# Units of 272 tokens per expert, with the second product transposed, in a fused attention, expert and GLU kernel

## The chip, the cores and the metric

The kernel runs on one core of a Trainium2 chip. The metric is the device time of one execution in microseconds (us). A core has a matrix engine (TensorE; its matmuls are the profile's PE, its weight loads PEld), a vector engine (VectorE, DVE), an activation engine (ScalarE, ACT), a general engine (GpSimd, POOL) and a queue that here only issues transfers (SyncE, SP). Each works through its own instructions in order, and semaphores make one wait for another.

## The reference

Attention inside chunks of 64 tokens, then a layer of eight experts, then a gated layer (GLU), on 4608 tokens of width 512:

```python
# attention: softmax(q k^T / 8) v in chunks of 64 tokens, giving x (4608 x 512)
do_compute = x @ w_skip > 0            # the other tokens pass unchanged
e_idx = argmax(x @ w_gate, axis=1)     # one expert per token
h = maximum(x[e] @ w1[e], 0)           # 512 -> 1024, per expert
x[e] += gate * (h @ w2[e])             # 1024 -> 512
out = (silu(x @ g_gate) * (x @ g_val)) @ g_out   # 512 -> 1536 -> 512
```

The inputs are drawn with seed 0. How many tokens go to each expert follows from them by the reference alone, without running the kernel:

| expert | 0 | 1 | 2 | 3 | 4 | 5 | 6 | 7 | sum |
|---|---|---|---|---|---|---|---|---|---|
| tokens | 271 | 252 | 388 | 506 | 104 | 266 | 237 | 266 | 2290 |
| of them among the first 3072 tokens | 206 | 125 | 257 | 435 | 77 | 191 | 163 | 232 | 1686 |

## The kernel before

Every float32 operand of a product is split into a high part and the rest, and a product is three matmuls that add up (`mm3`, L246 to L249: high by high, high by low, low by high). Weights are loaded by SP in halves of 512 KB (`st`, L134), four slices to a chunk. ACT rounds a slice to its high part (`whi`, L145), and DVE, or for each fourth slice POOL, subtracts (`wlo`, L147). Ten buffers hold five chunks of high and low parts. A unit of expert work needs four chunks.

**Slots.** While attention runs, the router gives each computed token a slot: expert number times 4608, plus its place among the tokens of that expert (L674 to L706). POOL scatters token number and gate to a table in DRAM, `perm`, at those slots (L709). A unit of work loads 128 entries of `perm` per tile of tokens (`pm`, L263), gathers the rows of X that they name (POOL, L276), and turns them for the matmuls on PE (`xpose`, L295 to L303).

**Static units** (`unit_static`) take the first UNIT = 256 slots of an expert. In eight steps over the hidden width, f = 0 to 7, the first product makes 128 hidden rows for 256 tokens (`hp`, weights stationary, 12 matmuls of 256 columns); ACT and DVE turn them into `hh` and `hl` (L351, L352); the second product of the step before adds to two tiles `y` (hidden rows stationary, weights moving, 6 matmuls of 512 columns). After step 7 `finish` (L308) computes x + gate * y.

**Dynamic units** (`unit_dyn`) take 128 further slots of whichever expert has them. Their place comes from a table `tab` that the kernel computes (`table`, L773 to L809): for each expert the tiles of 128 beyond UNIT slots, and their sum. NDYN = 7 of them stand in the program as written out code. If the sum is larger, a loop in the program (`For_i(NDYN, total, 1)`, L916 to L943) runs once for each further tile, with nothing else beside it. In the loop body SP loads `perm` and the four chunks of 1 MB, POOL gathers, and all 16 slices are split by ACT and POOL (L935, L936).

**The first unit** starts before routing is complete. It gathers only rows below 3072. So when the router has done the first 24 of 36 tiles of tokens (CUT, L693), it moves the counter of the first unit's expert up to UNIT if it is lower (`least`, L475): later tokens of that expert get slots from UNIT on. Before the change that expert is 0.

The order of the units is s0, s1, d0, s2, d1, ... s6, d5, s7, d6 with the last d5 and s7 exchanged (L118 to L121). The loop stands between the first unit and the second. All instructions are in an order written by hand: `tick(f)` (L955 to L985) issues, after step f of a unit, gathers, scatters, the turn of the next unit's rows and `pump` (splits of later weights). During static units it also prepares the first weights of the GLU (`gpump`, three DVE passes in L225 to L231).

Of the kernel before, what the change touches and what calls it, by code (L numbers as in the profile page):

```python
# [11 lines left out]
I32 = mybir.dt.int32  # L12
# [22 lines left out]
UNIT = 256  # L35
NDYN = NE - 1
# [14 lines left out]
def attention_moe_glu_kernel(  # L51
# [66 lines left out]
    units = [("s", 0)]  # L118
    for n in range(1, NE):
        units += [("s", n), ("d", n - 1)]  # L120
    units[-3:-1] = units[-2], units[-3]  # L121
# [151 lines left out]
    def gather(u, n=NT + 1):  # L273
        for r in rows[u]:
            x = al["x"](u)
            ins = nc.gpsimd.indirect_dma_start(  # L276
                out=x, out_offset=None, in_=X[0:n, :],
                in_offset=bass.IndirectOffsetOnAxis(ap=r[0][:, 0:1].bitcast(U32), axis=0),
                bounds_check=n - 1, oob_is_err=False,
            )  # L280
            apart(ins, u)
            r.append(x)


    def first_rows(u):
        rows[u] = []
        for t in range(2):
            x = al["x"](u)
            ins = nc.sync.dma_start(out=x, in_=X[t * P:(t + 1) * P, :])
            if not t:  # L290
                after(ins, [n for _, n in stored])
                stored.clear()
# [12 lines left out]
    def finish(u, ys):  # L305
        for (pm, x), y in zip(rows.pop(u), ys):
            o = al["o"](x)
# [16 lines left out]
    def unit_static(u, getc, donec, tail, tick, half=lambda f: None):  # L324
        xh, xl = xts.pop(u)
        ys = []

        def mm2(f, hh, hl):
            if f == 0:
                ys.extend(al["y"](t) for t in range(2))  # L330
            wh, wl = getc(2, f // 4)
            for t in range(2):
                ts = slice(t * P, (t + 1) * P)
                mm3(ys[t], hh[:, ts], hl[:, ts], wh[:, f % 4, :], wl[:, f % 4, :], f == 0, f == 7)
# [3 lines left out]
            if f == 7:  # L338
                finish(u, ys)

        for f in range(8):
# [13 lines left out]
            half(f)  # L355
            if tail:
                tail()
# [4 lines left out]
    def unit_dyn(u, getc, donec, tail, tick):  # L362
# [15 lines left out]
        def hpose(f2):  # L378
# [3 lines left out]
            hh = hp_[1].tile([P, 4, P], F32R, tag="hth", name="hth")  # L382
            hl = hp_[1].tile([P, 4, P], F32R, tag="htl", name="htl")
# [19 lines left out]
        if tail:  # L403
            tail()
        tick(0)
        mm1(1, (0, 1))
        tick(1)
# [11 lines left out]
    def pre_perm(u):  # L419
# [3 lines left out]
        if kind == "s":  # L423
            load_perm(u, [n * NT, n * NT + P])
# [7 lines left out]
    with ExitStack() as actx:  # L432
# [42 lines left out]
        nc.vector.memset(least[:, 0:1], float(UNIT))  # L475
# [242 lines left out]
        pm0 = [xtp.tile([P, 2], I32, name=f"pm{t}") for t in range(2)]  # L718
# [5 lines left out]
        for i in range(NTILE):  # L724
# [29 lines left out]
            if i == NTILE - 4:  # L754
                xs = x0p.tile([P, 2, DM], F32, name="x0")
                nc.gpsimd.memset(xs, 0.0)
                x0 = [xs[:, 0], xs[:, 1]]
            for n in range(2 if i < NTILE - LAG else len(pending)):
# [70 lines left out]
        def s0_tick(f):  # L829
# [17 lines left out]
            y=lambda t: ps_u.tile([P, DM], F32, tag="o", name="y"),  # L847
# [16 lines left out]
        around[0] = ps_u  # L864
        xt_p = ctx.enter_context(tc.tile_pool(name="xt", bufs=2, side="right"))
        mctx = ctx.enter_context(ExitStack())
        io = mctx.enter_context(tc.tile_pool(name="io", bufs=5, side="right"))
        hp_.append(mctx.enter_context(tc.tile_pool(name="h", bufs=3, side="right")))
# [19 lines left out]
        tail()  # L888
# [3 lines left out]
    with mctx:  # L892
# [57 lines left out]
        for u, (kind, n) in enumerate(units):  # L950
# [4 lines left out]
            def tick(f, u=u, kind=kind, nxt=nxt):  # L955
                if f == 1:
                    put()
                    if kind == "s":
                        gather(u + 1)
                if f == (5 if kind == "s" else 3) and nxt:  # L960
                    xpose(u + 1)
                if kind == "s":
# [7 lines left out]
                    if f == 6 and units[u + 1][0] == "d":  # L970
# [3 lines left out]
                if u == len(units) - 2 and f == 1:  # L974
# [26 lines left out]
    with ExitStack() as gctx:  # L1001
# [7 lines left out]
        sizes = [2, 2] + [BLK // P] * ((NT - 3 * UNIT) // BLK) + [2]  # L1009
# [140 lines left out]
```

## Time and profile before

| what | value |
|---|---|
| median of 3 runs | 1396.05 us (1394.64 to 1399.95) |
| the profiled execution | 1393.52 us |
| its span, first to last instruction | 1391.5 us |
| PE busy | 1314.6 us (94%) |
| DVE busy | 704.0 us (51%) |
| mean granted TensorE clock | 0.984 |

The span has four stretches: attention and routing with preparation to 161.1 us, the first unit and the check of the loop to 199.2 us, the other expert units to 473.2 us, and the GLU to the end. "Busy" of PE counts a matmul until its modelled end, and ends overlap the next start. The pace is therefore read from the distance of one start to the next. A row of the timeline gives the start, the duration, engine, line, operation, output and inputs, and what ended an idle time before it.

### The profile page before, as it was taken

To read this page: it belongs to the slowest core of one execution; us is meant where nothing else is said; L and a number is where in the kernel's file an instruction comes from. 1 tells how busy PE (TensorE), PEld (TensorE's weight loads), DVE (VectorE), ACT (ScalarE), POOL (GpSimd) and SP (SyncE) were. 2 spreads that over 40 slices of the span, in tenths; PEclk is the share of its full clock that TensorE was granted. 3 is DMA by queue.
4 is the path that set the end of the run, shared out by engine and by line. 5 is a ranking of instruction groups with operands and counts; after the bars stand their busy time and mean duration, and the time that the engine had idled before them with its cause. 6 is when DMAs were issued, how large, how long until landed. Compare 5 with 4: busy or idle time off the path is not lost.

```text
span 1391.5 us, 23406 instructions
## 1 busy us (share of the span) xinstructions
PE 1314.6 (94%) x9500; PEld 1190.1 (86%) x9500; DVE 704.0 (51%) x1207; ACT 450.7 (32%) x906; POOL 274.3 (20%) x233
## 2 busy tenths in 40 slices
PE   7766889999999899999999999999999999999998
PEld 6645678778778788999999999999999999999998
DVE  7755657998887788433332323333333333242322
ACT  4644435665665433311221212212121122121121
POOL 0333634555554466200000000000000000000000
PEclk9987989999999999999999999999999999999999
DMA  9998347888887745010202020201001020201000
GB/s 335 372 276 222 112 145 245 279 285 269 267 288 234 225 139 137 31 23 0 46 1 46 0 46 1 46 1 38 9 23 24 0 46 1 46 1 38 1 23 16
DMA packets 131855, 150.98 MB, mean 109 GB/s; under 512 B 78848, under 2 KB 79360, under 8 KB 131746
## 3 DMA queue, kind: packets, MB, share of 16 engines
q1 hardware_dynamic: 126914, 138.82, 32.6%
q0 software_dynamic: 4832, 10.65, 2.3%
q8 instruction: 75, 1.23, 0.4%
q14 instruction: 34, 0.28, 0.1%
HBM read 125.61 MB, written 25.28 MB: 108 GB/s over the span
## 4 chain that ended last, share of the span: by engine, by line
PE 69%; DVE 7%; issue 3%; DMA 2%; ACT 2%; POOL 2%; SPq 0%; DVEq 0%; ACTq 0%; POOLq 0%
PE o L249 7%; PE o L248 7%; PE o L247 7%; PE pg L249 6%; PE pg L247 6%; PE pg L248 6%; PE pv L247 6%; PE pv L248 6%; PE pv L249 6%; DVE wlo L147 3%; DMA st<-in_moe_w_dram 2%; ACT whi L145 2%; PE y L249 1%; PE y L247 1%; PE y L248 1%
## 5 line engine op out<-in xcount | busy, mean ns | idle before, releaser
L1091 DVE TENSOR_TENSOR sg<-pg,sg 128x384 f32<-128x384 f32 (+1 forms) x132 | 72.0, 546 | 327.0 <-ACT sg L1090 327.0
L1095 ACT ACTIVATE uh<-sg 128x384 fp32r<-128x384 f32 (+1 forms) x156 | 78.0, 500 | 311.8 <-DVE sg L1092 311.8
L249 PE MATMUL pg<-xh,glo 128*128 128x384 f32 (+1 forms) x528 | 175.7, 333 | 0.0
L247 PE MATMUL pg<-xh,ghi 128*128 128x384 f32 (+1 forms) x528 | 175.4, 332 | 0.0
L248 PE MATMUL pg<-xl,ghi 128*128 128x384 f32 (+1 forms) x528 | 175.0, 331 | 0.0
L247 PE MATMUL pv<-xh,ghi 128*128 128x384 f32 (+1 forms) x528 | 174.1, 330 | 0.0
L249 PE MATMUL pv<-xh,glo 128*128 128x384 f32 (+1 forms) x528 | 174.1, 330 | 0.0
L248 PE MATMUL pv<-xl,ghi 128*128 128x384 f32 (+1 forms) x528 | 174.1, 330 | 0.0
L249 PE MATMUL o<-ghi,ul 128*128 128x512 f32 x432 | 171.2, 396 | 2.2 <-POOL ul L1097 2.2
L247 PE MATMUL o<-ghi,uh 128*128 128x512 f32 x432 | 168.9, 391 | 2.6 <-ACT uh L1095 2.6
L248 PE MATMUL o<-glo,uh 128*128 128x512 f32 x432 | 170.8, 395 | 0.0
L1090 ACT ACTIVATE sg<-pg 128x384 f32<-128x384 f32 (+1 forms) x132 | 63.6, 482 | 312.7 <-PE pg L249 312.7
L147 DVE TENSOR_TENSOR wlo<-st,whi 128x512 fp32r<-128x512 f32 x165 | 151.0, 947 | 17.9 <-ACT whi L145 16.5
L145 ACT ACTIVATE whi<-st 128x512 fp32r<-128x512 f32 x240 | 137.7, 624 | 27.5 <-DMA st<-in_moe_w_dram 25.6
L147 POOL TENSOR_TENSOR wlo<-st,whi 128x512 fp32r<-128x512 f32 x75 | 101.4, 1352 | 156.4 <-ACT whi L145 142.0
L1092 DVE TENSOR_TENSOR sg<-pv,sg 128x384 f32<-128x384 f32 (+1 forms) x132 | 72.1, 546 | 118.6 <-PE pv L249 118.5
L1097 DVE TENSOR_TENSOR ul<-sg,uh 128x384 fp32r<-128x384 f32 (+1 forms) x132 | 72.2, 547 | 76.7 <-ACT uh L1095 76.7
L247 PEld LDWEIGHTS pg<-xh,ghi 128*128 128x128 f32 x528 | 99.5, 188 | 5.9
L248 PEld LDWEIGHTS pg<-xl,ghi 128*128 128x128 f32 x528 | 99.3, 188 | 5.7
L249 PEld LDWEIGHTS o<-ghi,ul 128*128 128x128 f32 x432 | 81.1, 188 | 21.6 <-POOL ul L1097 4.4
L249 PEld LDWEIGHTS pv<-xh,glo 128*128 128x128 f32 x528 | 99.4, 188 | 0.0
L248 PEld LDWEIGHTS pv<-xl,ghi 128*128 128x128 f32 x528 | 99.4, 188 | 0.0
(160 smaller groups left out, 2454.0 us busy)
## 6 DMA issues: line engine op xcount, KB each, us to landing
st<-in_moe_w_dram SPq DMA_DIRECT2D x120, 512.0 KB, 5.0
q<-in_qkv_dram SPq DMA_DIRECT2D x35, 768.0 KB, 9.8
X<-x SPq DMA_DIRECT2D x36, 256.0 KB, 9.7
out_dram<-os SPq DMA_DIRECT2D x36, 256.0 KB, 2.0
xr<-X SPq DMA_DIRECT2D x128, 64.0 KB, 2.6
gst<-in_moe_w_gate_dram SPq DMA_DIRECT2D x12, 512.0 KB, 4.1
gst<-in_moe_w_val_dram SPq DMA_DIRECT2D x12, 512.0 KB, 3.6
gst<-in_moe_w_out_dram SPq DMA_DIRECT2D x12, 512.0 KB, 3.7
```

The costliest lines, as they stand in the source:

```text
L145: nc.scalar.activation(out=hi[:, k, :], in_=stage[:, k % 2, :], func=ACTF.Copy)
L147: eng.tensor_tensor(out=lo[:, k, :], in0=stage[:, k % 2, :], in1=hi[:, k, :].bitcast(F32), op=ALU.subtract)
L247: nc.tensor.matmul(ps, ah, bh, start=start, stop=False)
L248: nc.tensor.matmul(ps, ah, bl, start=False, stop=False)
L249: nc.tensor.matmul(ps, al, bh, start=False, stop=stop)
L1090: nc.scalar.activation(out=u, in_=pg, func=ACTF.Sigmoid)
L1091: nc.vector.tensor_tensor(out=u, in0=pg, in1=u, op=ALU.mult)
L1092: nc.vector.tensor_tensor(out=u, in0=pv_, in1=u, op=ALU.mult)
L1095: nc.scalar.activation(out=uh, in_=u, func=ACTF.Copy)
L1097: eng.tensor_tensor(out=ul, in0=u, in1=uh.bitcast(F32), op=ALU.subtract)
```

## The change

A static unit has 272 slots: two tiles of 128 tokens and one of 16 (`rest`). The 16 rows of unit u lie in partitions from 32 * (u mod 4), and their table entries are loaded twice, once there and once at partition 0 as index for gather and scatter. The second product now has the weights stationary and the hidden rows moving: four tiles `yt` of 128 output columns by 272 tokens, 12 matmuls of 272 columns per step where there were 6 of 512. After the last step ACT copies the four tiles to `yts`, and in step 2 of the next unit PE turns them back in three groups (12 transposes, `turned`), after which `finish` adds into the gathered rows in place. For unit 0 this follows at once. The scatters move from tick 1 to tick 3 (tick 2 in a dynamic unit).

NDYN is 3. The order is expert 4 as first unit, then 0, 1, d0, 2, 3, 5, 6, 7, d1, d2; `least` holds for expert 4. Function and loop body of the dynamic units are the same, but for buffers. PSUM gives `yt` four single buffers, where `y` had two tiles of two buffers; the last of them also serves `y` of the dynamic units.

```diff
...
 RT = 4
-UNIT = 256
-NDYN = NE - 1
+UNIT = 272
+REST = UNIT - 2 * P
+FIRST = 4
+EXPERTS = [FIRST] + [e for e in range(NE) if e != FIRST]
+NDYN = 3
 TAB = 40
...
     ORDER_D = [(1, 0), (1, 1), (2, 0), (2, 1)]
-    units = [("s", 0)]
-    for n in range(1, NE):
-        units += [("s", n), ("d", n - 1)]
-    units[-3:-1] = units[-2], units[-3]
+    units = [("s", n) for n in EXPERTS]
+    for n, at in enumerate((3, 9, 10)):
+        units.insert(at, ("d", n))
     for kind, n in units:
...
+
+    def rest(u):
+        return slice(32 * (u % 4), 32 * (u % 4) + REST)
+
     def load_perm(u, bases):
         r = []
-        for b in bases:
+        for t, b in enumerate(bases):
             pm = al["pm"](u)
-            src = perm[b:b + P, :] if isinstance(b, int) else perm[bass.ds(b, P), :]
+            idx = pm
+            if t == 2:
+                src = perm[b:b + REST, :]
+                idx = al["pm"](u)[0:REST]
+                ins = nc.sync.dma_start(out=idx, in_=src)
+                after(ins, scattered)
+                pm = pm[rest(u)]
+            else:
+                src = perm[b:b + P, :] if isinstance(b, int) else perm[bass.ds(b, P), :]
             ins = nc.sync.dma_start(out=pm, in_=src)
             after(ins, scattered)
-            r.append([pm])
+            r.append([pm, idx])
         rows[u] = r
...
                 stored.clear()
-            rows[u].append([None, x])
+            rows[u].append([None, None, x])
...
         xh, xl = xts[u] = al["xt"](u)
-        for t, (_, x) in enumerate(rows[u]):
+        for t, (_, _, x) in enumerate(rows[u]):
             p = al["t"](t)
+            n = P
+            one = ident
+            if t == 2:
+                n = REST
+                one = ident[rest(u), rest(u)]
             for k in range(KD):
-                nc.tensor.transpose(p[:, k, :], x[:, k * P:(k + 1) * P], ident)
-            sl = slice(t * P, (t + 1) * P)
-            nc.scalar.activation(out=xh[:, :, sl], in_=p, func=ACTF.Copy)
-            nc.vector.tensor_tensor(out=xl[:, :, sl], in0=p, in1=xh[:, :, sl].bitcast(F32), op=ALU.subtract)
+                nc.tensor.transpose(p[:, k, 0:n], x[:, k * P:(k + 1) * P], one)
+            sl = slice(t * P, t * P + n)
+            nc.scalar.activation(out=xh[:, :, sl], in_=p[:, :, 0:n], func=ACTF.Copy)
+            nc.vector.tensor_tensor(
+                out=xl[:, :, sl], in0=p[:, :, 0:n], in1=xh[:, :, sl].bitcast(F32), op=ALU.subtract
+            )
     def finish(u, ys):
-        for (pm, x), y in zip(rows.pop(u), ys):
-            o = al["o"](x)
+        for (pm, idx, x), y in zip(rows.pop(u), ys):
+            o = x
+            if u == 0:
+                o = al["x"](u) if y.shape[0] == P else al["xr"][rest(u)]
             nc.vector.scalar_tensor_tensor(
...
             )
-            outs.append((u, pm, o))
+            outs.append((u, idx, o))
...
         while outs:
-            u, pm, o = outs.pop(0)
+            u, idx, o = outs.pop(0)
             ins = nc.gpsimd.indirect_dma_start(
-                out=X, out_offset=bass.IndirectOffsetOnAxis(ap=pm[:, 0:1].bitcast(U32), axis=0),
+                out=X, out_offset=bass.IndirectOffsetOnAxis(ap=idx[:, 0:1].bitcast(U32), axis=0),
                 in_=o, in_offset=None, bounds_check=NT - 1, oob_is_err=False,
...
         xh, xl = xts.pop(u)
-        ys = []
+        ys, back = [], None
         def mm2(f, hh, hl):
-            if f == 0:
-                ys.extend(al["y"](t) for t in range(2))
             wh, wl = getc(2, f // 4)
-            for t in range(2):
-                ts = slice(t * P, (t + 1) * P)
-                mm3(ys[t], hh[:, ts], hl[:, ts], wh[:, f % 4, :], wl[:, f % 4, :], f == 0, f == 7)
+            for d in range(KD):
+                if f == 0:
+                    ys.append(al["yt"](d))
+                ds = slice(d * P, (d + 1) * P)
+                mm3(ys[d], wh[:, f % 4, ds], wl[:, f % 4, ds], hh, hl, f == 0, f == 7)
             if f % 4 == 3:
...
                 donec(2, f // 4)
-            if f == 7:
-                finish(u, ys)
+            if f < 7:
+                return None
+            ts = []
+            for d in range(KD):
+                if d % 2 == 0:
+                    ts.append(al["ts"]())
+                nc.scalar.activation(out=ts[-1][:, d % 2, :], in_=ys[d], func=ACTF.Copy)
+
+            def turned():
+                ps = []
+                for t in range(3):
+                    p = al["t"](t)
+                    q, n = (p, P) if t < 2 else (p[0:REST], REST)
+                    for d in range(KD):
+                        nc.tensor.transpose(q[:, d, :], ts[d // 2][:, d % 2, t * P:t * P + n], ident)
+                    ps.append(q.rearrange("p k d -> p (k d)"))
+                    if t == 1:
+                        r = rows[u]
+                        rows[u] = r[:2]
+                        finish(u, ps)
+                        rows[u] = r[2:]
+                finish(u, ps[2:])
+
+            return turned
...
             half(f)
+            if f == 2 and back:
+                back()
             if tail:
-                tail()
+                back = tail() or back
             tail = lambda f=f, hh=hh, hl=hl: mm2(f, hh, hl)
...
         nc.vector.tensor_copy(least, base)
-        nc.vector.memset(least[:, 0:1], float(UNIT))
+        nc.vector.tensor_scalar(least[:, FIRST:FIRST + 1], least[:, FIRST:FIRST + 1], float(UNIT), None, op0=ALU.add)
         pair = xtp.tile([P, NTILE, 2], I32, name="pair")
...
             h=lambda n: ps_u.tile([P, n], F32, tag="s", name="hp"),
-            y=lambda t: ps_u.tile([P, DM], F32, tag="o", name="y"),
+            yt=lambda d: ps_u.tile([P, UNIT], F32, tag=f"y{d}", name="yt", bufs=1),
+            ts=lambda: ts0.tile([P, 2, UNIT], F32, tag="ts", name="yts"),
         )
...
         ps_u = actx.enter_context(tc.tile_pool(name="ps_u", bufs=2, space=PSUM))
+        ts0 = actx.enter_context(tc.tile_pool(name="ts0", bufs=2))
         al.update(
-            pm=lambda u: io.tile([P, 2], I32, tag="pm", name="pm", bufs=8),
+            pm=lambda u: io.tile([P, 2], I32, tag="pm", name="pm", bufs=18),
             x=lambda u: io.tile([P, DM], F32, tag="x", name="x"),
+            xr=io.tile([P, DM], F32, tag="xr", name="xr", bufs=1),
-            o=lambda x: io.tile([P, DM], F32, tag="o", name="o", bufs=2),
         )
         xpose(0)
-        x0 = [x for _, x in rows[0]]
+        x0 = [r[2] for r in rows[0]]
         pre_perm(0)
...
         gpool["st"] = mctx.enter_context(tc.tile_pool(name="gst", bufs=1))
-        hp_.append(mctx.enter_context(tc.tile_pool(name="hd", bufs=2)))
+        hp_.append(mctx.enter_context(tc.tile_pool(name="hd", bufs=4)))
-        ps_y = mctx.enter_context(tc.tile_pool(name="ps_y", bufs=2, space=PSUM))
+        ps_y = mctx.enter_context(tc.tile_pool(name="ps_y", bufs=1, space=PSUM))
         ps_t = mctx.enter_context(tc.tile_pool(name="ps_t", bufs=2, space=PSUM))
...
             h=lambda n: ps_h.tile([P, n], F32, tag="h", name="hp"),
-            y=lambda t: ps_y.tile([P, DM], F32, tag=f"y{t}", name=f"y{t}"),
+            yt=lambda d: ps_y.tile([P, UNIT], F32, tag=f"y{d}", name="yt"),
+            ts=lambda: hp_[1].tile([P, 2, UNIT], F32, tag="hd", name="yts"),
+            y=lambda t: ps_y.tile([P, DM], F32, tag="y3", name="y"),
         )
         usual = dict(al)
-        held = [outs.pop(0) for _ in range(2)]
+        held = outs[:]
+        outs.clear()
         al.update(
             pm=lambda u: io.tile([P, 2], I32, tag="lpm", name="lpm", bufs=1),
-            o=lambda x: x,
             x=lambda u: gpool["st"].tile([P, DM], F32, tag="st", name="lx"),
...
             def tick(f, u=u, kind=kind, nxt=nxt):
-                if f == 1:
+                if f == (3 if kind == "s" else 2):
                     put()
-                    if kind == "s":
-                        gather(u + 1)
+                if f == 1 and kind == "s":
+                    gather(u + 1)
                 if f == (5 if kind == "s" else 3) and nxt:
...
```

PE, near the end of expert 6's static unit, before: the last matmuls of a step's second product (`y`), the turn of the next unit's rows (`tp<-ident,x`), the next step (`hp`).

```order
L247 MATMUL y_5767<-whi,hh 128x512
L248 MATMUL y_5767<-wlo,hh 128x512
L249 MATMUL y_5767<-whi,hl 128x512
L247 MATMUL y_5768<-whi,hh 128x512
L248 MATMUL y_5768<-wlo,hh 128x512
L249 MATMUL y_5768<-whi,hl 128x512
L300 MATMUL tp<-ident,x 128x128 x8
L247 MATMUL hp<-xh,whi 128x256
```

The same place after the change (the line numbers of `mm3` are two higher; the first two of the four column tiles are left out):

```order
L249 MATMUL yt<-hh,whi 128x272
L250 MATMUL yt<-hl,whi 128x272
L251 MATMUL yt<-hh,wlo 128x272
L249 MATMUL yt<-hh,whi 128x272
L250 MATMUL yt<-hl,whi 128x272
L251 MATMUL yt<-hh,wlo 128x272
L319 MATMUL tp<-ident,x 128x128 x8
L319 MATMUL tp<-ident,xr 128x16 x4
L249 MATMUL hp<-xh,whi 128x272
```

A third group of four transposes stands between the eight and the next step, and `tp` has two buffers as before.

PE, in step 2 of expert 7's static unit, after the change: the end of the first product (`hp`), the turn back of expert 6's result (`yts`), the second product of step 1.

```order
L251 MATMUL hp<-xh,wlo 128x272
L375 MATMUL tp<-ident,yts 128x128 x8
L375 MATMUL tp<-ident,yts 16x128 x4
L249 MATMUL yt<-hh,whi 128x272
L250 MATMUL yt<-hl,whi 128x272
```

Before, the second product followed the first here with nothing between.

POOL, the body of the loop and what follows it, after the change (`lx` and `wl` are the loop's rows and weights; the branch at its end is L968):

```order
L290 DMA lx<-X,lpm 128x512
L988 TENSOR_TENSOR wl_lo<-wl,wl_hi 128x512 x16
L339 DMA X<-lx,lpm 4609x512
L968 REGISTER_ALU
L968 COMPARE_AND_BRANCH
L968 UNCONDITIONAL_BRANCH
L339 DMA X<-x,pm 4609x512 x2
L339 DMA X<-xr,pm 4609x512
L290 DMA x<-X,pm 128x512 x2
L290 DMA xr<-X,pm 16x512
```

The body is as before; after it three scatters and three gathers follow, where two scatters and one gather (of a dynamic unit) stood.

## Rows read from the trace of the kernel before

**Rows 1.** The page's busy times: us, share of the span, instructions.
```profile
PE 1314.6 (94%) x9500; PEld 1190.1 (86%) x9500; DVE 704.0 (51%) x1207; ACT 450.7 (32%) x906; POOL 274.3 (20%) x233
```

**Rows 2.** Windows: stretch, length; PE, PEld, DVE, ACT, POOL busy; PEclk, DMA share, GB/s.
```profile
161.10:199.20 38.10, 31.38 (x211) 26.50 (x209) 22.10 (x65) 10.91 (x24) 16.59 (x16) 0.91 0.42 129
199.20:442.50 243.30, 229.57 (x1354) 199.32 (x1355) 208.15 (x281) 149.47 (x298) 129.92 (x98) 0.99 0.79 266
442.50:473.20 30.70, 27.48 (x131) 21.69 (x130) 19.57 (x29) 18.25 (x33) 11.22 (x9) 1.00 0.77 256
```

**Rows 3.** Timeline of PE: first matmuls of s1, d4, s6, d5 and the GLU.
```profile
199.19 0.45 PE L247 MATMUL hp<-xh,whi 128*128 128x256 f32 x1 [2.15 <-issue]
...
379.57 0.40 PE L247 MATMUL hp<-whi,xh 128*128 128x512 f32 x1
...
392.62 0.28 PE L247 MATMUL hp<-xh,whi 128*128 128x256 f32 x1
...
442.54 0.40 PE L247 MATMUL hp<-whi,xh 128*128 128x512 f32 x1
...
473.21 0.28 PE L247 MATMUL pgv<-xh,ghi 128*128 128x256 f32 x1
```

**Rows 4.** Timeline of PE inside a static unit, and one DVE row.
```profile
281.26 0.28 PE L247 MATMUL hp<-xh,whi 128*128 128x256 f32 x1
281.38 0.28 PE L248 MATMUL hp<-xl,whi 128*128 128x256 f32 x1
...
282.70 0.40 PE L247 MATMUL y<-whi,hh 128*128 128x512 f32 x1
282.94 0.39 PE L248 MATMUL y<-wlo,hh 128*128 128x512 f32 x1
...
294.28 0.60 PE L300 MATMUL tp<-ident,x 128*128 128x128 f32 x4
294.63 0.37 PE L247 MATMUL hp<-xh,whi 128*128 128x256 f32 x1
...
295.54 0.69 DVE L303 TENSOR_TENSOR xl<-tp,xh 128x512 fp32r<-128x512 f32 x1 [0.82 <-ACT xh L302]
```

**Rows 5.** Waits of PE, 220 to 460 us: total, times, longest.
```profile
PE y L249 <- DVE hl L352: 8.8, 8, 1.9
```

**Rows 6.** The page's queue of POOL's transfers: packets, MB, share.
```profile
q0 software_dynamic: 4832, 10.65, 2.3%
```

**Rows 7.** DMA issues by line: count, KB each, median us to landing.
```profile
st<-in_moe_w_dram SPq DMA_DIRECT2D x120, 512.0 KB, 5.0
...
pm<-perm SPq DMA_DIRECT2D x25, 1.0 KB, 3.7
x<-X,pm POOLq DMA_INDIRECT x23, 5.1
X<-o,pm POOLq DMA_INDIRECT x23, 4.9
```

**Rows 8.** Instructions of tiles wlo, whi and o: ns min/median/max, first and last start.
```profile
L147 POOL TENSOR_TENSOR wlo<-st,whi x75: 1265/1305/1814, 36.8 to 468.8; 128x512 fp32r<-128x512 f32 x75
...
L145 ACT ACTIVATE whi<-st x240: 612/623/647, 36.1 to 468.1; 128x512 fp32r<-128x512 f32 x120
...
L308 DVE SCALAR_TENSOR_TENSOR o<-y,pm,x x23: 733/746/753, 193.5 to 473.7; 128x512 f32<-128x512 f32 x23
```

**Rows 9.** Timeline of PE at the end of the first unit.
```profile
189.03 1.07 PE L300 MATMUL xp<-ident,x 128*128 128x128 f32 x4 [2.37 <-DMA x<-X,pm]
191.00 1.12 PE L300 MATMUL xp<-ident,x 128*128 128x128 f32 x4 [0.90 <-DMA x<-X,pm]
191.77 0.78 PE L247 MATMUL y<-whi,hh 128*128 128x512 f32 x1
...
194.48 2.55 PE L460 MATMUL wu<-ones 128*128 128x128 bf16 x30
```

More of the change, by code (lines that the diff above doesn't have):

```diff
@@ L273, in gather @@
     def gather(u, n=NT + 1):
-        for r in rows[u]:
-            x = al["x"](u)
+        for t, r in enumerate(rows[u]):
+            x = al["x"](u) if t < 2 else al["xr"][rest(u)]
             ins = nc.gpsimd.indirect_dma_start(
                 out=x, out_offset=None, in_=X[0:n, :],
-                in_offset=bass.IndirectOffsetOnAxis(ap=r[0][:, 0:1].bitcast(U32), axis=0),
+                in_offset=bass.IndirectOffsetOnAxis(ap=r[1][:, 0:1].bitcast(U32), axis=0),
                 bounds_check=n - 1, oob_is_err=False,
@@ L381, in hpose @@
                 nc.tensor.transpose(p[:, f, :], hs[f2][:, f * P:(f + 1) * P], ident)
-            hh = hp_[1].tile([P, 4, P], F32R, tag="hth", name="hth")
-            hl = hp_[1].tile([P, 4, P], F32R, tag="htl", name="htl")
+            hh = hp_[1].tile([P, 4, P], F32R, tag="hd", name="hth")
+            hl = hp_[1].tile([P, 4, P], F32R, tag="hd", name="htl")
             nc.scalar.activation(out=hh, in_=p, func=ACTF.Copy)
@@ L402, in unit_dyn @@
         mm1(0, (0, 1, 2, 3))
-        if tail:
-            tail()
+        back = tail() if tail else None
         tick(0)
         mm1(1, (0, 1))
+        if back:
+            back()
         tick(1)
@@ L423, in pre_perm @@
         if kind == "s":
-            load_perm(u, [n * NT, n * NT + P])
+            load_perm(u, [n * NT, n * NT + P, n * NT + 2 * P])
         else:
@@ L716, in scatter @@
             scattered.append(ins.ins.name)
-        pm0 = [xtp.tile([P, 2], I32, name=f"pm{t}") for t in range(2)]
+        pm0 = [xtp.tile([P, 2], I32, name=f"pm{t}") for t in range(4)]
         al["pm"] = lambda u: pm0.pop(0)
@@ L754, in attention_moe_glu_kernel @@
             if i == NTILE - 4:
-                xs = x0p.tile([P, 2, DM], F32, name="x0")
+                xs = x0p.tile([P, 3, DM], F32, name="x0")
                 nc.gpsimd.memset(xs, 0.0)
                 x0 = [xs[:, 0], xs[:, 1]]
+                al["xr"] = xs[:, 2]
             for n in range(2 if i < NTILE - LAG else len(pending)):
@@ L863, in attention_moe_glu_kernel @@
         ps_u = actx.enter_context(tc.tile_pool(name="ps_u", bufs=2, space=PSUM))
-        around[0] = ps_u
         xt_p = ctx.enter_context(tc.tile_pool(name="xt", bufs=2, side="right"))
         mctx = ctx.enter_context(ExitStack())
-        io = mctx.enter_context(tc.tile_pool(name="io", bufs=5, side="right"))
-        hp_.append(mctx.enter_context(tc.tile_pool(name="h", bufs=3, side="right")))
+        io = mctx.enter_context(tc.tile_pool(name="io", bufs=6, side="right"))
+        hp_.append(mctx.enter_context(tc.tile_pool(name="h", bufs=2, side="right")))
+        ts0 = actx.enter_context(tc.tile_pool(name="ts0", bufs=2))
         al.update(
-            pm=lambda u: io.tile([P, 2], I32, tag="pm", name="pm", bufs=8),
+            pm=lambda u: io.tile([P, 2], I32, tag="pm", name="pm", bufs=18),
             x=lambda u: io.tile([P, DM], F32, tag="x", name="x"),
+            xr=io.tile([P, DM], F32, tag="xr", name="xr", bufs=1),
             xt=lambda u: [xt_p.tile([P, KD, BLK], F32R, tag=nm, name=nm) for nm in ("xh", "xl")],
-            o=lambda x: io.tile([P, DM], F32, tag="o", name="o", bufs=2),
         )
         xpose(0)
-        x0 = [x for _, x in rows[0]]
+        x0 = [r[2] for r in rows[0]]
         pre_perm(0)
@@ L887, in attention_moe_glu_kernel @@
         )
-        tail()
+        tail()()
         warm_up(30, ps_u, "s")
@@ L969, in tick @@
                         gsplit()
-                    if f == 6 and units[u + 1][0] == "d":
+                    if f == 6 and units[u + 1][0] == "d" and u + 2 < len(units):
                         gather(u + 2)
@@ L973, in tick @@
                     pump(2)
-                if u == len(units) - 2 and f == 1:
+                if u == len(units) - 2 and f == 3:
                     first_rows("a")
@@ L1006, in attention_moe_glu_kernel @@
         ps_o = gctx.enter_context(tc.tile_pool(name="ps_o", bufs=1, space=PSUM))
-        sizes = [2, 2] + [BLK // P] * ((NT - 3 * UNIT) // BLK) + [2]
+        sizes = [2, 2] + [BLK // P] * ((NT - 3 * GT) // BLK) + [2]
         first = [0]
```

## The prediction

> **What bounds the kernel now.** I read the shares first: PE is busy 94% of the span, DVE 51% [rows 1]. A mean over unlike stretches says little, so the windows come next [rows 2]. The change touches the first unit (161.1 to 199.2 us) and the other expert units (199.2 to 473.2 us); the 918 us of GLU behind them keep their instructions. In the expert units PE is busy 229.6 of 243.3 us, DVE 208.2, and the transfers take 0.79 of the DMA engines' time: three resources near their limits. The starts on PE tell which one sets the pace. In a static unit matmuls of 256 columns start every 0.12 us and those of 512 every 0.23 to 0.24 us, back to back over whole steps [rows 4]; 96 x 0.12 + 48 x 0.23 = 22.6 us. Two static units in a row took 392.62 to 442.54 us [rows 3], 24.96 us each; the rest is 8 transposes (four in 0.35 us [rows 4]) and 1.7 us of stalls, such as PE waiting for DVE's `hl`, 8.8 us in 8 waits [rows 5]. So static units are bound by PE, with small waits. A dynamic unit took 379.57 to 392.62 us, 13.05 us; the last two, with the way into the GLU, 442.54 to 473.21 us, 30.7 us [rows 3].
>
> **How many further tiles there are.** This decides the case. By the counts per expert, UNIT = 256 leaves 1, 0, 2, 2, 0, 1, 0, 1 tiles, expert 0 counted as 256 + 65, for its first unit holds early tokens only. The sum is 7 = NDYN, and the loop isn't entered. The trace bears out the counts: 206 + 7 x 256 + 7 x 128 = 2894 gathered rows and 2290 scattered ones are 5184 x 2,048 bytes, with 36 x 128 table entries of 8 bytes 10.65 MB, what POOL's queue moved [rows 6].
>
> With UNIT = 272 expert 2 has 116 tokens beyond it, one tile, and expert 3 has 234, two tiles. The others have none, except the first unit's expert. That is now expert 4. It has 77 tokens among the first 3072, so its counter is moved up to 272, and its 27 late tokens get slots 272 to 298: one more tile. The sum is 4, NDYN is 3, and the loop runs once. (With expert 3 first, 435 early ones, it would be 3.) So the change removes four dynamic units from the written-out program and adds one to the loop.
>
> **The loop, once.** Nothing of it is in this trace, so it is put together from rows. All engines meet before it; no prefetch and no other unit lies beside it. The chain: SP reads two table words into registers and loads `perm` (1.2 us, an estimate, and 3.7 us), POOL gathers (5.1 us) [rows 7]. Turn, copy and the first rounding on ACT, each some 0.6 us [rows 4, 8]: 1.8 us. Then 16 POOL subtractions of 1.305 us [rows 8]: 20.9 us, since POOL alone does them and PE, ACT and DVE wait for them slice by slice. Twice POOL waits in turn: ACT rounds the next chunk only behind the Relu of the product that needed POOL's last slice, some 2 us each, 4 us. Behind the last slice two matmuls at the low clock, `finish` 0.75 us [rows 8], and the scatter to its landing, 4.9 us [rows 7], which the engines wait for at the loop's end: 6.3 us. The weights (5.0 us per half chunk [rows 7]) land beside this. The way out of the loop costs another meeting, for which I take the 2.15 us that PE lost at the check of the loop that wasn't entered [rows 3]. Sum: 1.2 + 3.7 + 5.1 + 1.8 + 20.9 + 4 + 6.3 + 2.15 = 45 us. From below: without register loads, POOL's waits and way out, 38 us. From above: chunks 3 and 4 wait for their buffers and then for two halves of 5 us each: 45 + 12 = 57 us. I take 45 us, since nearly all of it has rows of its own.
>
> The Trainium skill's page "Runtime: NRT & Kernel Launch" (Instruction fetch mechanics) says that a taken branch out of the fetched window stalls for an instruction fetch. The 2.15 us of PE at the skipped loop, with "issue" named as its cause [rows 3], agree with that. By the rule a loop that is entered runs straight on into its body and out of it, and would not pay this twice: the total below would be 2 us lower.
>
> **A static unit.** 192 matmuls of 272 columns. Between 0.12 us at 256 and 0.23 us at 512 columns, 272 take 0.1266 us: 24.3 us, 1.7 us more than before. To this come two places where PE stands on a buffer:
> - `xpose` turns three tiles through two PSUM buffers. The third waits until DVE has read the first. Before, four transposes started at 294.28 us and DVE's `xl` of them ended at 296.23 us [rows 4], 1.95 us. So the third group starts some 2.15 us after the first and ends at 2.6 us. Before, two groups took 0.9 us.
> - `turned` likewise: third group behind the first `finish`, which in DVE's order stands behind `hl` of step 2. Hand-over 0.1, Relu 0.4, `hl` 0.4, `finish` 0.75 [rows 8], 0.2 back to PE, transposes 0.45: 2.3 us per unit, all new. The mm2 of step 1 and all later matmuls queue behind it on PE, and ACT's next Relu waits for them.
>
> ACT's copies of `yt` are hidden by step 1 of the next unit. DVE has per unit fewer splits than before, 16 slices in 29 us instead of 32 in 39 us, so its `hl` should come in time. Sum 24.3 + 2.6 + 2.3 = 29.2 us. From below, if both waits were hidden and the groups ran through: 26.9 us. From above, each wait behind one of DVE's slow splits and the `hl` waits back: 32 us. I take 29.2 us, the sum of the rows.
>
> **Expert units after the first.** Seven static units 204.4 us; 1.5 us for the start at the low clock (0.45 us for the first matmul [rows 3]), which before has too; d0 13.05 us and 1.85 us for the third tile of unit 2 and for `finish` holding a buffer; the last two 31 us. Together 252 us instead of 274.0 us (199.19 to 473.21): 22 us saved. From below 233 us (41 saved), from above 274 us (nothing).
>
> **The first unit.** Its longer steps lie under the wait of 2.37 us for the gather [rows 9]. But a third gather and third turn stand before the last product: from 191.77 us to some 193.4 us, +1.6 us. Then 12 matmuls of 272 columns at the low clock, 2.9 instead of 2.7 us (191.77 to 194.48), and exposed, before warm-up matmuls and loop, four copies and three groups of transposes with their wait: 3 us. Together 5 us (2 to 9).
>
> The scatters' move by two steps costs nothing: a step takes 3 us, the rows are awaited only at the GLU's second block, and POOL has 113 of 243 us free [rows 2]. The additional `perm` loads are 1 KB or less each.
>
> **Sum.** + 45 + 5 - 22 = + 28 us. The profiled execution took 1393.5 us, 2.5 us under the median of 1396.05 us; the change gives 1421.5 us against the one and 1424 us against the other. I predict 1424 us.
>
> **Rivals.**
> - *The loop isn't entered.* If the table's sum is 3 or less, 45 us fall away: 1379 us, faster. It decides at the 27 late tokens of expert 4; for it speaks only that three tiles were written out, against it the counts that the trace confirms to the row [rows 6]. 4%.
> - *DVE and transfers, not PE, set the units.* Then PE's new work disappears in waits that go away with four units' weights. Static units stay at 24.96 us: 7 x 4.2 us less, 1394 us, no change. For it speaks 208 of 243 us of DVE [rows 2]; against it that PE runs back to back over whole steps [rows 4]. 6%.
> - *The two buffer waits are hidden*, static units take 26.9 us: 1424 - 16 - 3 for d0 and the end = 1405 us. It needs DVE to read the first buffer within the 0.8 us of two groups, and rows 4 show 1.95 us. 13%.
> - *The loop is longer*, 57 us, because its weights come late: 1436 us. For it: third and fourth chunk need buffers of the first two. 15%.
>
> **How the numbers follow.** The forecast itself has 62%. A measurement of this kernel tells about 0.5%, 7 us, from no change: 1389 to 1403 us. Faster is the loop not entered and a small part of the second rival: 5%. Same: most of the second and the low end of the third, 9%. Slower: 86%. With the bounds of the terms (loop 38 to 57, expert units -41 to 0, first unit 2 to 9) the range that leaves two in ten out is 1402 to 1441 us.
>
> **What the new profile would show.** Rows on the loop's lines, 16 POOL subtractions in a row, and PE nearly idle for some 45 us between two static units; without them the forecast is wrong by just that. Static units of 29 us from first `hp` to first `hp`, in each a gap of about 1.3 us before the third group of `tp` ended by DVE `xl`, and one before the third group of turns ended by `finish`; without those gaps the third rival holds. Matmuls of 272 columns at 0.127 us. The GLU should take 918 us again; if it doesn't, I have missed something there.

## The result and the profile after

The changed kernel took 1411.14 us, the median of seven runs (1406.86 to 1420.83), and the kernel before beside it 1396.05 us (1390.93 to 1403.52). The ratio is 1.0107, with a 95% interval from 1.0073 to 1.0142: slower by 15 us. The forecast was slower by 28 us, 1424 us in a range from 1402 to 1441. The sign and the cause were right, and the price was 13 us too high.

The profiled execution of the changed kernel is the longest of its seven, 1420.83 us (span 1419.1 us). Its first expert unit began at 173.1 us, that of the kernel before at 161.1 us [rows 2], and a second profile of the kernel before (experiment 7) began it at 167.95 us. In front of it the diff adds the turn of the first unit's third tile, which also stands 0.98 us on a buffer: some 1.5 us (169.00 to 171.64 us from the turn's start to PE's next work, against 165.90 to 167.04 us in that second profile). The forecast had put nothing for it. The rest differs from one execution to the next, so the comparison starts at the first unit.

The windows of the changed kernel, which answer to [rows 2]: stretch, length; PE, PEld, DVE, ACT, POOL busy; PEclk, DMA share, GB/s.

```profile
173.08:207.61 34.53, 32.33 (x245) 30.36 (x243) 18.79 (x59) 12.42 (x29) 14.92 (x14) 0.92 0.37 119
207.61:251.57 43.96, 23.71 (x92) 15.10 (x90) 3.73 (x6) 11.28 (x21) 22.01 (x18) 0.75 0.30 103
251.57:501.02 249.45, 233.36 (x1688) 220.57 (x1689) 169.19 (x258) 134.06 (x281) 119.21 (x96) 0.97 0.67 221
501.02:1419.10 918.08, 908.92 (x5049) 849.47 (x5047) 347.50 (x594) 194.90 (x393) 61.11 (x49) 1.00 0.13 32
```

The four stretches are the first unit, the loop, the other expert units and the GLU. By [rows 2, 3, 9] the same stretches of before are 33.4 us (161.10 to 194.48), 4.7 us (194.48 to 199.19), 274.0 us (to 473.21) and 918.3 us. So the first unit costs 1.1 us more, the loop 39.3 more, the other units 24.6 less: +15.8 us, near the 15.1 us of the medians. The agreement is partly luck: against the second profile of the kernel before the same terms are +4.9, +40.0 and -22.8 us, together +22.1. The loop and the other units repeat within 2 us; the first unit doesn't (experiment 7). In the second stretch PE is busy for 23.7 of 44 us, warm-up matmuls included, and POOL for 22.0.

The page's row of POOL's queue of transfers, which answers to [rows 6]: packets, MB, share.

```profile
q0 software_dynamic: 4864, 9.83, 1.9%
```

The bytes fit four further tiles: 77 rows gathered by the first unit, 7 x 272 by the others and 4 x 128 by the tiles are 2493; with the 2290 scattered rows 4783 x 2,048 bytes, and with the table's 0.04 MB 9.83 MB. That a fourth tile was run is seen in the timeline of PE, from the end of the first unit to the next one: start, us, engine, line, operation, tiles, count, and in brackets the idle time before it with what ended it.

```profile
207.61 1.84 PE L508 MATMUL wu<-ones 128*128 128x128 bf16 x30
217.12 1.09 PE L319 MATMUL tp<-ident,lx 128*128 128x128 f32 x4 [7.67 <-DMA lx<-X,lpm]
...
251.57 0.60 PE L249 MATMUL hp<-xh,whi 128*128 128x272 f32 x1 [4.79 <-issue]
```

`lx` and `lpm` are tiles of the loop's body, and `hp<-xh,whi` is the next static unit: the loop ran once. Inside it, the timeline of POOL:

```profile
209.72 1.04 POOL L290 DMA_INDIRECT lx<-X,lpm  x1 [5.08 <-PE wu L508]
219.50 4.98 POOL L988 TENSOR_TENSOR wl_lo<-wl,wl_hi 128x512 fp32r<-128x512 f32 x4 [8.74 <-ACT wl_hi L987]
227.11 4.99 POOL L988 TENSOR_TENSOR wl_lo<-wl,wl_hi 128x512 fp32r<-128x512 f32 x4 [2.63 <-ACT wl_hi L987]
235.12 4.97 POOL L988 TENSOR_TENSOR wl_lo<-wl,wl_hi 128x512 fp32r<-128x512 f32 x4 [3.02 <-ACT wl_hi L987]
240.98 5.00 POOL L988 TENSOR_TENSOR wl_lo<-wl,wl_hi 128x512 fp32r<-128x512 f32 x4 [0.89 <-ACT wl_hi L987]
247.84 1.03 POOL L339 DMA_INDIRECT X<-lx,lpm  x1 [1.86 <-DVE lx L331]
```

Four groups of four subtractions, 20 us, with gaps of 2.63, 3.02 and 0.89 us in which POOL waits for ACT: the spine of the 44 us. The chain of work that ended last shows the way out: the scatter from its issue to its landing, and what lies between that and the next unit.

```profile
247.84 2.33 DMA X<-lx,lpm
250.18 1.39 issue
```

A static unit of the changed kernel, in the timeline of PE, from its first product to that of the next (it answers to [rows 4]):

```profile
382.43 0.29 PE L249 MATMUL hp<-xh,whi 128*128 128x272 f32 x1
...
403.16 1.03 PE L319 MATMUL tp<-ident,x 128*128 128x128 f32 x8
405.18 0.41 PE L319 MATMUL tp<-ident,xr 16*128 16x16 f32 x4 [0.98 <-DVE xl L322]
...
411.66 0.29 PE L249 MATMUL hp<-xh,whi 128*128 128x272 f32 x1
...
419.61 1.03 PE L375 MATMUL tp<-ident,yts 128*128 128x128 f32 x8
421.39 0.60 PE L375 MATMUL tp<-ident,yts 128*16 128x128 f32 x4 [0.75 <-DVE x L331]
...
440.82 0.29 PE L249 MATMUL hp<-xh,whi 128*128 128x272 f32 x1
```

These two units take 29.23 and 29.16 us (forecast 29.2). Both third groups stand behind a named wait, for `xl` and for `finish` (`x`, line 331), the two stalls of the forecast.

### The profile page after: what moved, and what is told of

Its sections match the earlier page's. It is cut to its first block, busy times and chain, and to the rows that moved or that the text cites. A ratio compares the mean times of both kernels' runs of the same rounds, so it can differ in the third digit from the quotient of the medians.

```text
span 1419.1 us, 23896 instructions
## 1 busy us (share of the span) xinstructions
PE 1324.8 (93%) x9832; PEld 1213.0 (85%) x9832; DVE 647.6 (46%) x1163; ACT 430.1 (30%) x883; POOL 275.8 (19%) x243
## 3 DMA queue, kind: packets, MB, share of 16 engines
q0 software_dynamic: 4864, 9.83, 1.9%
## 4 chain that ended last, share of the span: by engine, by line
PE 70%; DVE 4%; issue 3%; ACT 2%; DMA 2%; POOL 2%; SPq 0%; POOLq 0%; DVEq 0%; ACTq 0%
PE o L251 7%; PE o L250 7%; PE o L249 7%; PE pg L251 6%; PE pg L249 6%; PE pg L250 6%; PE pv L251 6%; PE pv L250 6%; PE pv L249 6%; PE yt L250 1%; PE hp L249 1%; PE hp L251 1%; PE hp L250 1%; PE yt L251 1%; PE yt L249 1%
## 5 line engine op out<-in xcount | busy, mean ns | idle before, releaser
L149 POOL TENSOR_TENSOR wlo<-st,whi 128x512 fp32r<-128x512 f32 x59 | 78.1, 1324 | 154.9 <-ACT whi L147 90.3
L149 DVE TENSOR_TENSOR wlo<-st,whi 128x512 fp32r<-128x512 f32 x117 | 93.2, 824 | 29.7 <-ACT whi L147 22.8
L147 ACT ACTIVATE whi<-st 128x512 fp32r<-128x512 f32 x176 | 101.5, 623 | 10.3 <-DMA st<-in_moe_w_dram 10.3
L249 PEld LDWEIGHTS pv<-xh,ghi 128*128 128x128 f32 x528 | 99.3, 188 | 0.0
```

Of the source, the lines that this page charges most:

```text
L147: nc.scalar.activation(out=hi[:, k, :], in_=stage[:, k % 2, :], func=ACTF.Copy)
L149: eng.tensor_tensor(out=lo[:, k, :], in0=stage[:, k % 2, :], in1=hi[:, k, :].bitcast(F32), op=ALU.subtract)
L249: nc.tensor.matmul(ps, ah, bh, start=start, stop=False)
```

## The experiments

The theory: the loss is the one pass through the loop, which costs far more than a written-out tile; static units are bound by PE, and each pays for two third groups that stand on a buffer. The rivals: the loss lies in the new form of the second product, or in the first unit, and DVE or the transfers set the period, so that PE's extra work is free and PE's savings come to nothing. "s1" below is the first static unit behind the loop.

**1. Expert 3 first.** With 435 early tokens it leaves no late fourth tile.

```
-FIRST = 4
+FIRST = 3
```

> Expert 3 instead of expert 4 as first unit, nothing else changed: the table then holds 3 further tiles and the loop isn't entered. Theory (the loop costs what the trace shows between the last warm-up matmul and the first matmul of the next unit, 42.1 us against 2.2 us without it): 1411 - 40 = 1371 us, 1.8% faster than before. Rival (the work of the fourth tile and its 4 MB of weights are what costs, a loop of its own costs little): 1411 - 13 = 1398 us, the same as before.

Measured: 1372.58 us (1371.71 to 1377.19), ratio 0.982 [0.9793, 0.9846]. Against the changed kernel that is 0.0287 of 1396, 40 us. Timeline of PE: warm-up, s1 and the GLU's first product.

```profile
205.20 1.84 PE L508 MATMUL wu<-ones 128*128 128x128 bf16 x30
...
209.08 0.39 PE L249 MATMUL hp<-xh,whi 128*128 128x272 f32 x1 [2.04 <-issue]
...
457.43 0.28 PE L249 MATMUL pgv<-xh,ghi 128*128 128x256 f32 x1
```

From warm-up to s1 there are 3.9 us instead of 44.0, and s1 to the GLU is 248.35 us against 249.45. POOL's queue moved 9.97 MB, which are 272 + 7 x 272 + 3 x 128 gathered rows and the 2290 scattered ones: three tiles. One number of the program, which moves 27 tokens, turns the change from 1.1% slower to 1.8% faster. The loss is the loop.

**2. The fourth tile written out.**

```
-NDYN = 3
+NDYN = 4
-    for n, at in enumerate((3, 9, 10)):
+    for n, at in enumerate((3, 6, 10, 11)):
```

> Expert 4 stays first, but four dynamic units are written out (NDYN = 4), so the fourth tile is done as a written-out unit and the loop isn't entered. Theory (the loop is dear because nothing lies beside it): 1371 us of the kernel without a fourth tile plus one dynamic unit of 13 to 15 us = 1385 us. Rival (a fourth tile costs the same wherever it stands): 1411 us as the changed kernel.

Measured: 1383.6 us (1379.26 to 1388.38), ratio 0.9902 [0.9871, 0.9932]. With experiment 1 this prices the fourth tile: 11 us written out (1383.6 - 1372.6), 40 us in the loop. It is the tile's place that is dear, not the tile.

**3. The loop's subtractions on DVE.** Is POOL the spine of the loop?

```
-                        nc.gpsimd.tensor_tensor(
+                        nc.vector.tensor_tensor(
```

> The changed kernel, with the 16 subtractions of the loop on DVE instead of POOL. Theory (they pace the loop: four take 5.0 us on POOL, on DVE some 0.69 us each, 2.8 us per chunk, with ACT's four roundings of 2.2 us before): 4 x 2.1 = 8 us less, 1403 us. Rival (transfers, meetings of the engines and the way in and out pace it): 1411 us.

Measured: 1407.4 us (1404.49 to 1410.59), ratio 1.0068 [1.0043, 1.0093], whose interval overlaps that of the changed kernel; the times alone don't decide. Timeline of DVE in the loop:

```profile
211.30 2.48 DVE L988 TENSOR_TENSOR wl_lo<-wl,wl_hi 128x512 fp32r<-128x512 f32 x4
218.28 2.50 DVE L988 TENSOR_TENSOR wl_lo<-wl,wl_hi 128x512 fp32r<-128x512 f32 x4 [4.50 <-ACT wl_hi L987]
...
```

Four take 2.5 us instead of 5.0, and from warm-up to s1 (199.85 to 235.8 us) there are 36.0 us instead of 44.0: 8 us less, as expected, of the 10 that POOL lost. The rest of the loop doesn't hang on POOL's speed.

**4. Two written-out tiles, the loop twice.**

```
-NDYN = 3
+NDYN = 2
-    for n, at in enumerate((3, 9, 10)):
+    for n, at in enumerate((8, 9)):
```

> The changed kernel with NDYN = 2: expert 4 first, two dynamic units written out (both at the end), so the loop runs twice. Theory (an iteration costs some 45 us in full, and the first costs 40 only because SP's load of its table entries ran ahead under the end of the first unit): 1411 - 11 (one written-out unit less) + 45 = 1445 us, with a second iteration longer than the first by the 4 to 5 us of that load. Rival (most of the 40 us are paid once, for entering the loop): 1411 - 11 + 25 = 1425 us.

Measured: 1443.54 us (1441.06 to 1449.1), ratio 1.0322 [1.0282, 1.0362], 32 us over the changed kernel (30 us by the two ratios), which has one pass fewer and one written-out tile more. Timelines of PE, of SP's queue and of POOL:

```profile
203.25 1.84 PE L508 MATMUL wu<-ones 128*128 128x128 bf16 x30
...
211.81 1.09 PE L319 MATMUL tp<-ident,lx 128*128 128x128 f32 x4 [6.72 <-DMA lx<-X,lpm]
...
258.51 1.09 PE L319 MATMUL tp<-ident,lx 128*128 128x128 f32 x4 [17.30 <-DMA wl<-in_moe_w_dram]
...
293.24 0.60 PE L249 MATMUL hp<-xh,whi 128*128 128x272 f32 x1 [4.82 <-issue]
```

```profile
200.89 0.37 SPq L277 DMA_DIRECT2D lpm<-perm  x1
...
249.47 0.35 SPq L277 DMA_DIRECT2D lpm<-perm  x1
```

```profile
242.28 1.03 POOL L339 DMA_INDIRECT X<-lx,lpm  x1 [1.86 <-DVE lx L331]
251.98 1.02 POOL L290 DMA_INDIRECT lx<-X,lpm  x1 [8.67 <-DMA lpm<-perm]
```

A pass from turn to turn takes 46.7 us, near the forecast's 45. The first is cheaper: SP waits for nothing in front of the loop and loads its `lpm` at 200.89 us, before the warm-up even starts (203.25), while the second `lpm` stands in the middle of the chain: scatter at 242.28, `lpm` at 249.47, gather at 251.98, turn at 258.51 us.

**5. The third groups moved apart.** On experiment 1: the third group of `xpose` one step later, the third group of turned results behind the next second product; each alone (`xsplit`, `tsplit`) and both.

```
...
-                back()
+                back(0)
...
-                back = tail() or back
+                t2 = tail()
+                if f == 2 and back:
+                    back(1)
+                back = t2 or back
...
-                    xpose(u + 1)
+                    xpose(u + 1, 0)
+                if f == (6 if kind == "s" else 4) and nxt:
+                    xpose(u + 1, 1)
```

> Expert 3 first, and only the third group of the turn of the next unit's rows moved one step later. Theory: the 1.49 us stall before it goes, 0.26 us for a second start of transposes comes, 7 x 1.2 = 8 us less than with expert 3 first (1372.6 us), 1364 us. Rival (DVE sets the pace, only the turn back matters): 1372 us.

Measured: 1363.2 us (1359.79 to 1369.72), ratio 0.9765 [0.9722, 0.9808].

> Expert 3 first, and only the third group of the turn back moved behind the second product of step 1. Theory: the 1.25 us stall goes, 0.26 us comes, 5 x 1.0 = 5 us less than with expert 3 first (1372.6 us), 1367 us. Rival (the wait comes back in full as one of PE for hl): 1372 us.

Measured: 1365.19 us (1361.34 to 1367.6), ratio 0.9773 [0.9734, 0.9812].

> As the kernel with expert 3 first, and the third group of four transposes moved away from the first two: of the turn of the next unit's rows one step later, of the turn back behind the second product that follows it (static units only). Theory (PE stands about 1.0 us on a buffer in each turn and 0.75 us in each turn back, and some 0.3 us restart): 7 x 1.3 + 5 x 1.0 = 14 us less than with expert 3 first, 1357 us. Rival (DVE sets the pace and the time comes back as waits for hl): no change, 1371 us.

Measured: 1362.03 us (1358.9 to 1363.22), ratio 0.9745 [0.9719, 0.9771]: 2.55% faster than the kernel before, the best of all versions. By the times only both together are clear of experiment 1 (0.9793 and 0.9771 are the near ends of the two intervals); each edit by itself overlaps. By the traces, from the first unit's first product to the GLU's, it is 284.0 us without, 277.1 and 277.6 with one, 271.4 with both: -6.9, -6.4 and -12.6, so they nearly add up. PE's waits between s1 and the GLU (line and tile, waited for, us in total, times, longest), first in experiment 1, then with both edits:

```profile
PE tp L375 <- DVE x L331: 6.1, 7, 1.6
PE tp L319 <- DVE xl L322: 6.0, 6, 1.2
...
PE yt L250 <- DVE hl L397: 1.8, 5, 0.8
```

```profile
PE yt L250 <- DVE hl L402: 3.9, 6, 1.2
...
PE tp L379 <- DVE x L335: 1.5, 2, 0.8
```

The 12.1 us on the two buffers fall to 1.5, and 2.1 us come back as waits for `hl`. A unit then takes 27.5 us, not the 26.9 that would be left without any stall:

```profile
324.84 0.28 PE L249 MATMUL hp<-xh,whi 128*128 128x272 f32 x1
...
335.48 0.60 PE L379 MATMUL tp<-ident,yts 128*16 128x128 f32 x4
...
348.93 0.42 PE L323 MATMUL tp<-ident,xr 16*128 16x16 f32 x4
...
352.38 0.28 PE L249 MATMUL hp<-xh,whi 128*128 128x272 f32 x1
```

If DVE or the transfers had set the period, it would have stayed at 29.2.

**6. The transposed second product alone**, with UNIT = 256, expert 0 first, seven written-out tiles in the old order and two tiles per unit.

```
-UNIT = 272
+UNIT = 256
-FIRST = 4
+FIRST = 0
-NDYN = 3
+NDYN = NE - 1
...
-                for t in range(3):
+                for t in range(2):
...
```

> The transposed second product alone: units of 256 tokens, expert 0 first, seven dynamic units in the order of the kernel before, no third tile. Theory (static units are bound by PE): per unit 96 x (2 x 0.12 - 0.235/2 - 0.12) = 0.4 us for the columns and 1.05 us for eight transposes back, 8 units, and 2 us exposed behind the first unit: + 13 us, 1410 us or 1.0% over the kernel before. Rival (a pair of a static and a dynamic unit is bound by DVE and the transfers, and PE's additions fill its waits): within 3 us of the kernel before.

Measured: 1404.91 us (1396.0 to 1409.69, twelve runs), ratio 1.0052 [1.0026, 1.0077]: +7 us, between the two expectations. The trace tells why. First products on PE of the static units s2, s3, s6 and s7 and of the dynamic unit behind s7; a dynamic unit stands between the static ones, except between s6 and s7:

```profile
244.44 0.28 PE L250 MATMUL hp<-xh,whi 128*128 128x256 f32 x1
...
284.02 0.28 PE L250 MATMUL hp<-xh,whi 128*128 128x256 f32 x1
...
404.06 0.28 PE L250 MATMUL hp<-xh,whi 128*128 128x256 f32 x1
...
431.28 0.28 PE L250 MATMUL hp<-xh,whi 128*128 128x256 f32 x1
...
455.83 0.39 PE L250 MATMUL hp<-whi,xh 128*128 128x512 f32 x1
```

And of the kernel before s2, s3 and s7 (s1, s6 and the last dynamic unit are in [rows 3]):

```profile
235.13 0.28 PE L247 MATMUL hp<-xh,whi 128*128 128x256 f32 x1
...
274.29 0.28 PE L247 MATMUL hp<-xh,whi 128*128 128x256 f32 x1
...
419.51 0.28 PE L247 MATMUL hp<-xh,whi 128*128 128x256 f32 x1
```

The pair of a static and a dynamic unit from s2 to s3 takes 39.6 us, against 39.2 before. All five pairs, from s1 (206.92 and 199.19 us) to s6, take 197.1 us against 193.4: +3.7 us of the 7.3 that 1.45 us for each would make. So about half of PE's new work fills waits there. The static unit behind a static one, s7, goes from 23.0 to 24.55 us: there 1.5 us, all of it, is paid. Neither theory holds everywhere. The 24.96 us of the prediction are the mean of two unlike units, s6 with 26.9 us, which has the end of a dynamic unit and a wait of 1.9 us for `hl` in it, and s7 with 23.0.

**7. The kernel before, profiled again**, with no edit.

> The kernel before once more, to see how far its first stretch differs from one execution to the next. In its first profile the first unit began at 161.1 us, in that of the changed kernel at 173.1 us, and in those of the other kernels between 164.0 and 173.4 us. Theory (attention and routing vary with the granted clock, and the change has no part in it): some time between 161 and 174 us, with the stretch from there to the GLU at 312 us and the GLU at 918 us again. Rival (the change delays the first unit): 161 us again.

Measured: 1395.61 us. Timeline of PE: first unit, warm-up, GLU.

```profile
167.95 0.39 PE L247 MATMUL hp<-xh,whi 128*128 128x256 f32 x1
...
197.55 1.85 PE L460 MATMUL wu<-ones 128*128 128x128 bf16 x30
...
473.76 0.28 PE L247 MATMUL pgv<-xh,ghi 128*128 128x256 f32 x1
```

The first unit began 6.85 us later than in the first profile, and the span grew by 2.0 us only: from the first unit's start to the GLU it took 305.8 us instead of the 312 expected. Windows of the first unit, as in [rows 2]: the kernel before in its first and in this profile, and experiment 1.

```profile
161.10:194.48 33.38, 28.81 (x180) 24.11 (x179) 21.35 (x64) 10.91 (x24) 15.50 (x15) 0.92 0.46 143
```

```profile
167.95:197.55 29.60, 26.66 (x181) 22.68 (x179) 19.20 (x64) 10.90 (x24) 12.58 (x12) 1.00 0.43 142
```

```profile
173.44:205.20 31.76, 29.87 (x245) 28.02 (x244) 19.43 (x63) 12.51 (x29) 15.03 (x14) 1.00 0.42 134
```

The length goes with the granted clock: 33.4 us at 0.92 and 29.6 us at 1.00 before, 34.5 us at 0.92 in the changed kernel and 31.7 to 32.9 us at 1.00 in the six profiles of experiments 1, 2, 3 and 5. So at like clock the first unit costs 1.1 us more at 0.92 and 2.1 to 3.3 us more at 1.00, with one profile of the kernel before at each. A few us in the first stretch can't be put down to the change by one profile.

## Why the prediction was right, and where it was off

**How many further tiles there are.** Right, and decisive. The loop was entered once (PE and POOL timelines), and without the 27 late tokens it isn't (experiment 1). The first rival falls, and its price was near: 1379 us forecast, 1372.58 measured.

**The loop, once: +45.** The term that was mis-sized. It measured +39.3 us by the traces and 40 by experiment 1. By its parts:
- Register loads, `perm` and gather were 10 us in the sum. From the warm-up's end to the first transpose it was 7.7 us (209.45 to 217.12): SP had loaded `lpm` beforehand (at 203.22 us), so the 3.7 and 1.2 us were not in the chain, but the gather took 7.4 us from its issue at 209.72, not 5.1, while the loop's first weights, which the forecast let land beside it at no price, kept the DMA engines busy (last section). The 1.2 us for register loads were an estimate that no row shows. In the second pass of experiment 4, where SP doesn't run ahead, the order of the forecast's chain holds, with 2.5 us for `lpm` and 6.5 for the gather.
- Middle, 1.8 + 20.9 + 4 = 26.7 us forecast: from 217.12 to the end of POOL's last subtraction at 245.98, 28.9 us. The subtractions were right (20 us); POOL's three gaps were 6.5 us instead of 4.
- End and way out, 8.45 us forecast: 5.6 us (245.98 to 251.57). The scatter landed 2.33 us after its issue, not 4.9 us [rows 7], and from its landing to the next unit's first product it was 1.39 us, not 2.15. The Trainium skill's page "Runtime: NRT & Kernel Launch" (Instruction fetch mechanics) says that a taken branch out of the fetched window stalls. The loop that was entered took 0.27 us from the warm-up's end to the gather's issue (209.45 to 209.72) and 1.39 us behind its scatter, together less than the 2.15 us of the skipped one [rows 3]; that the 2.15 us aren't paid twice agrees with the page, but no row shows what the 1.39 us consist of. The forecast named the rule and summed without it; by it the 45 us would have been 43.
- These parts make 42.1 us, from the warm-up's end to the next unit. Against the kernel before they count 40.0, since it stands 2.15 us in the same place for the loop that it skips, and 39.3 with its longer warm-up (2.55 against 1.84 us). The forecast set all of its 45 us against nothing. About half of the 5.7 us of the miss is this, the other half are the parts.

**A static unit, 29.2 us.** Right where a unit has both third groups: 28.7, 29.2 and 29.2 us. But the sum took 29.2 us for all seven static units, and four are unlike: the first has nothing to turn back (27.6 us), the two in front of a dynamic unit have no third tile to turn for it (27.1 and 27.2), and the one behind d0 has the end of d0 and a wait of 2.1 us for `hl` in it (31.6). Matmuls of 272 columns start every 0.125 us (198.28, 198.40, 198.53 and 198.65 us), against 0.1266. The third group of `xpose` started 2.02 us behind the first (forecast 2.15). Experiment 5 shows that both stalls were real and could be taken out.

**Expert units after the first: -22.** Measured -24.6 (-22.8 against the second profile of the kernel before). The seven static units took 200.7 us instead of 205.9 with the start at the low clock; d0 took 15.8 us instead of 14.9, and the last two 33.0 us instead of 31. So two errors of unlike sign partly cancel.

**The first unit: +5.** It measured +1.1 us between the two first profiles, but at the full granted clock 2.1 to 3.3 us (experiment 7), and the 1.5 us of the third turn in front of it, which the forecast left out, come on top. The wait for the gather of 2.37 us [rows 9] did shrink, to 0.4 us in the changed kernel (PE's wait of `xp` for `x`), and the third turn waits 0.98 us for `xl`. What the third gather and turn cost by themselves stays open.

By the first profiles the errors of the terms, 5.7 us in the loop, 3.9 in the first unit and 2.6 in the other units, are 12.2 of the 13 us; of these only the loop's is the same within a us against either profile of the kernel before.

**Rivals.** The second (DVE and transfers set the units) is refuted where it was asked, in static units behind each other (experiment 5), and right by about half in the pairs of the old order (experiment 6), which the forecast had not told apart. The third (waits hidden) is refuted by the two gaps with their named causes. The fourth (57 us) needed late weights; in the first pass nothing waited for them by the rows of PE and POOL, and in the second the row of PE names `wl` for its 17.30 us (experiment 4), but what starts there is the turn of `lx`, whose gather POOL had issued at 251.98 us. From turn to turn it took no more than 46.7 us.

The GLU took 918.1 us, against 918.3 in the first profile of the kernel before and 919.7 in the second.

## What to carry to other kernels

Where data decide how often a loop in the program runs, count from the data what a new tile size leaves for it, before counting what is saved: one pass cost 40 us here, the same tile written out 11. A third small group through two buffers stalls an engine that is otherwise busy throughout, and putting other work between the groups takes the stall out (2.55% instead of 1.8% faster here). Work that is added to the bounding engine is priced stretch by stretch, since it costs less where it fills a wait.

## What the runs showed that was not expected

- SP runs ahead: it loaded the loop's table entries at 200.89 us and PE came to the warm-up in front of the loop at 203.25 (experiment 4). A queue that waits for nothing takes part of a loop's first pass out of its chain.
- A single gather in the loop took 7.4 us from issue to use, and 6.5 to 6.9 us in the passes of experiments 3 and 4, where the median of all gathers before was 5.1 us to landing [rows 7]. While it was under way the DMA engines were busy for 0.89 of the time (309 GB/s), with the first 2 MB of the loop's weights issued at 209.48 us, just before it. That the weights slow the gather fits, but no run takes them away.
- The granted clock was 0.75 over the loop and 0.97 to 1.00 behind it. The stretch in front of the first unit took 161.1 to 166.2 us in the five profiles with a granted clock of 0.89 or more from 10 us on, and 167.5 to 173.4 us in the six with less. Whether the clock is its cause isn't settled.
